# Eight groups of a weight product ahead of the experts in place of five, and a later store of the soft maxima

## The chip, the cores and the metric

One Trainium2 chip, one of its cores. The metric is the device time of one execution in microseconds; the kernel before has a median of 406.53 us in 3 runs.

The core has five engines that run their own instruction streams: TensorE (PE, with its weight loads shown as PEld), VectorE (DVE), ScalarE (ACT), GpSimd (POOL) and SyncE (SP, which issues nearly all transfers here). Matmul results go to eight PSUM banks, all else lies in on-chip tiles or in DRAM.

## What is computed

Three layers follow one another, in float32: a retention attention over 8 batches, 8 heads, 576 positions and 64 features; a soft mixture of 8 experts with 4 slots each over the 4608 tokens; and a bilinear layer.

```python
def _attn_ref(q, k, v):                      # scores weighted by Dmat, then times v
    ...
    ret = scores * Dmat[None, :, :, :]
    return np.matmul(ret, v)

def _moe_ref(x, phi, w1, w2):
    logits = x @ phi                         # 4608 x 32
    d = np.exp(logits - logits.max(0));  d /= d.sum(0) + 1e-09
    slot_input = d.T @ x
    for e in range(E):
        h = np.maximum(slot_input[e] @ w1[e], 0.0)
        slot_out[e] = h @ w2[e]
    ...
    c = np.exp(logits - logits.max(1));  c /= c.sum(1) + 1e-09
    return c @ slot_out

def _moe2_ref(x, w1, w2, w3, w_out):
    a = x @ w1
    b = x @ w2
    h = a * b @ w3
    return h @ w_out
```

w3 and w_out are 64-bit in DRAM, and so are the two projections w1 and w2 of the bilinear layer; the kernel turns them into 32-bit values itself.

## The kernel before

**Stages.** A loop over 36 units of 128 tokens does the attention and, beside it, the logits, running soft maxima over the tokens and the slots' sums. A passage behind it finishes the maxima: the normalisers, and `slotm`, the experts' input. A loop over the 8 experts follows. Behind it the slots' outputs are turned (`acc`, `sot`), multiplied by the two projections (L985), multiplied pairwise (VectorE, L1029 to L1036), and multiplied by W (L1044). The last loop writes 36 blocks of 128 tokens (L1110 to L1125), with coefficients made from the soft maxima over the slots.

**W, the product of the weights.** W = w3 x w_out does not depend on the data, so its matmuls are put wherever `emit_Ws(n)` is called: n groups of three matmuls of 128x512 each (high by high, high by low, low by high part; L557). There are 64 groups, 4 for each of 16 blocks of w3 and 8 for each of 8 blocks of W. A block of w3 is loaded (L472), converted on ScalarE, VectorE and GpSimd (L490 to L516), cast to its high part on ScalarE (L521) and split on GpSimd (L526) into one of three places in `w3p`. A place is written again when its four groups are done. Each eighth group ends a block of W, which is evicted at the next `tick()`: a cast on ScalarE (L565) and a subtraction on VectorE (L566).

**Where the groups stand.** Three and then five behind the attention; in the experts' loop as many as a count that rises with the step lets through (up to 52, and three more in the last expert); three, two and four behind the loop.

**An expert.** `emit_l1(e)`: 32 matmuls (L593) with four tiles of 512 KB of w1. ScalarE makes `hr` (L598), VectorE turns it into `ht` (L605), and `emit_l2(e)`: 16 matmuls (L612) with four tiles of w2. The tiles' places come free with these matmuls, and `load_expert` puts the next loads on SP (L576) into free places. SP issues in program order; each transfer also waits for the one that stands eight before it on SP.

**The passage ahead of the experts.** ScalarE casts two blocks of w3 (L521), each as soon as its place is read for the last time by the product's groups, and then brings `zacc` up to date (L434). VectorE makes `zb` from it (L874) and, behind that, the last sum `acc` (L451). TensorE's matmuls with `zb` (L875) and `acc` (L881) follow, then the first expert's first layer.

**The soft maxima over the slots.** In the experts' loop nine steps (`soft`) fill `et`. `store_expt` writes it to DRAM (`expt`) in 16 transfers on SP (L416), and `load_pairs` reads it back (L624 to L626) into `lga`, `raw` and `vals`, 12 transfers for each of 9 blocks. `pair_prep` makes the coefficients; its first product for the first block is on GpSimd (L638), its cast on ScalarE (L639).

## Time and profile before

| | before |
|---|---|
| median of 3 runs | 406.53 us (404.79 to 406.96) |
| the profiled execution's own time | 406.82 us |
| its span | 405.1 us |
| TensorE busy | 382.5 us (94%) |
| VectorE, ScalarE, GpSimd busy | 260.7, 199.8, 172.1 us (64%, 49%, 42%) |
| moved | 108.75 MB, 268 GB/s in the mean |

TensorE is busy nearly throughout, but that share is a mean over stages with different limits. The views that tell them apart are the chain that ended last, the order of each engine's instructions in time with the idle time ahead of each and what ended it, and short stretches with the clock that TensorE was granted and the share of the transfer engines. Their rows stand further below.

### The profile page before, as it was taken

How to read it: one execution, taken by the hardware profiler on the slowest of the kernel's cores; microseconds unless marked ns; L12 is line 12 of the kernel's file. 1: busy time of each engine (PE TensorE's matmuls, PEld its weight loads, DVE VectorE, ACT ScalarE, POOL GpSimd, SP SyncE). 2: the span in 40 equal slices, each digit the busy share in tenths (PEclk: the TensorE clock that was granted, in tenths of full speed). 3: DMA queues.
4: the chain of work that ended last, by engine and by line, in shares of the span. 5: the costliest groups of instructions: out<-in, count | busy, mean ns of one | idle time of the engine just before them, and what ended most of it. 6: DMA issues, size and time to landing. Idle time of an engine off the chain costs nothing.

```text
span 405.1 us, 10964 instructions
## 1 busy us (share of the span) xinstructions
PE 382.5 (94%) x4447; PEld 286.0 (71%) x4447; DVE 260.7 (64%) x432; ACT 199.8 (49%) x424; POOL 172.1 (42%) x158
## 2 busy tenths in 40 slices
PE   6999988998999998979999898999999999999996
PEld 3888676877878886555565354567877777787774
DVE  3457999998888998426874572179866444455500
ACT  2346695777667785315454322045345445452532
POOL 2632777564264545022643342034734345543520
PEclk9999999999999999989999899999999999999999
DMA  7999898799979888996999999593076998999634
GB/s 234 308 333 322 266 367 299 226 353 391 304 239 331 331 266 301 310 404 243 391 406 407 411 407 409 163 211 77 2 171 154 238 223 229 220 216 235 154 84 104
DMA packets 48211, 108.75 MB, mean 268 GB/s; under 512 B 7584, under 2 KB 10016, under 8 KB 48160
## 3 DMA queue, kind: packets, MB, share of 16 engines
q1 hardware_dynamic: 47008, 107.85, 83.6%
q8 instruction: 35, 0.57, 0.6%
q10 hardware_dynamic: 1152, 0.20, 0.3%
q14 instruction: 16, 0.13, 0.1%
HBM read 97.41 MB, written 10.62 MB: 267 GB/s over the span
## 4 chain that ended last, share of the span: by engine, by line
PE 43%; DMA 7%; DVE 2%; ACT 1%; issue 0%; ACTq 0%; DVEq 0%; SPq 0%
PE bank L1119 9%; PE bank L1121 8%; PE bank L1120 8%; PE bank L557 5%; PE bank L1044 5%; DMA v<-in_ew 3%; DMA kt<-in_ew 3%; PE bank L612 2%; DMA k<-in_ew 2%; PE bank L593 2%; PE bank L1110 2%; PE bank L1074 1%; PE bank L985 1%; DVE w L566 0%; ACT w L565 0%
## 5 line engine op out<-in xcount | busy, mean ns | idle before, releaser
L636 POOL TENSOR_TENSOR cc<-mw_sb,cc 128x512 fp32r<-128x512 f32 x36 | 46.0, 1297 | 56.1 <-ACT cc L635 56.1
L516 POOL TENSOR_TENSOR vals<-vals,msb 128x512 int32<-128x512 int32 x24 | 30.8, 1284 | 57.7 <-DVE vals L490 37.2
L557 PE MATMUL bank<-wop,w3p 128*128 128x512 f32 x192 | 52.0, 414 | 0.0
L557 PEld LDWEIGHTS bank<-wop,w3p 128*128 128x128 f32 x192 | 35.3, 194 | 15.7 <-issue 9.0
L263 DVE TENSOR_TENSOR pm<-scores,msb 128x1024 f32<-128x1024 f32 x31 | 37.8, 1219 | 12.8 <-PE scores L253 12.5
L635 ACT CAST cc<-mw_sb 128x512 fp32r<-128x512 f32 x36 | 22.2, 616 | 43.6 <-DVE mw_sb L634 34.8
L1119 PE MATMUL bank<-w3p,cc 128*128 128x512 f32 x108 | 43.1, 399 | 0.0
L1121 PE MATMUL bank<-w3p,cc 128*128 128x512 f32 x108 | 42.1, 390 | 0.0
L1120 PE MATMUL bank<-w3p,cc 128*128 128x512 f32 x108 | 42.0, 389 | 0.0
L253 PE MATMUL scores<-q,kt 64*128 64x128 f32 x496 | 37.3, 290 | 0.0
L634 DVE TENSOR_TENSOR mw_sb<-lga,raw 128x512 f32<-128x512 f32 x32 | 29.3, 955 | 12.3 <-POOL cc L636 12.1
L282 PE MATMUL output<-pm,v 128*64 128x128 f32 x512 | 35.2, 279 | 1.1 <-issue 1.0
L526 POOL TENSOR_TENSOR w3p<-vals,w3p 128x512 fp32r<-128x512 f32 x16 | 20.5, 1283 | 33.7 <-ACT w3p L521 33.7
L1123 ACT ACTIVATE mw_sb<-bank,rz 128x512 f32<-128x512 f32 x36 | 24.7, 685 | 20.1 <-PE bank L1121 11.3
L516 POOL TENSOR_TENSOR mw_sb<-mw_sb,msb 128x512 int32<-128x512 int32 x16 | 20.4, 1277 | 32.0 <-DVE mw_sb L490 22.4
L253 PEld LDWEIGHTS scores<-q,kt 64*128 64x128 f32 x496 | 31.1, 192 | 3.0 <-issue 1.1
L282 PEld LDWEIGHTS output<-pm,v 128*64 128x64 f32 x512 | 27.4, 136 | 6.3 <-issue 4.5
L192 POOL TENSOR_TENSOR k<-kr,msb 128x512 f32<-128x512 f32 (+1 forms) x30 | 26.3, 897 | 5.3 <-DMA kr<-in_v 3.1
L220 ACT COPY kt<-pair 128x512 f32<-128x512 f32 x26 | 15.3, 587 | 26.0 <-PE pair L219 26.0
L497 ACT ACTIVATE msb<-raw 128x512 int32<-128x512 uint32 x40 | 27.9, 698 | 0.0
L316 PE MATMUL output<-q,st 64*64 64x128 f32 (+1 forms) x512 | 20.1, 268 | 6.5 <-DVE xts L327 4.5
L1119 PEld LDWEIGHTS bank<-w3p,cc 128*128 128x128 f32 x108 | 20.3, 188 | 7.1 <-issue 2.9
(226 smaller groups left out, 777.1 us busy)
## 6 DMA issues: line engine op xcount, KB each, us to landing
q<-in_q SPq DMA_DIRECT2D x20, 512.0 KB, 6.4
raw<-expt SPq DMA_DIRECT2D x36, 256.0 KB, 4.2
kr<-in_v SPq DMA_DIRECT2D x16, 512.0 KB, 6.2
v<-in_v SPq DMA_DIRECT2D x16, 512.0 KB, 6.7
raw<-in_m SPq DMA_DIRECT2D x16, 512.0 KB, 5.9
raw<-in_w SPq DMA_DIRECT2D x16, 512.0 KB, 6.3
out_x<-mw_sb SPq DMA_DIRECT2D x64, 128.0 KB, 2.4
k<-in_ew SPq DMA_DIRECT2D x14, 512.0 KB, 10.1
```

Of the source, the lines that this page charges most:

```text
L192: (nc.vector if first else nc.gpsimd).tensor_tensor(out=Ks[:, :, 0:m, h], in0=K[:, 1 - h, :, 0:m], in1=ktab(c, h)[:, 0:m].unsqueeze(1).uns ...
L253: last = nc.tensor.matmul(out=ps[:, p], lhsT=ktb[u % 2][a, p], rhs=Q[a, :, x, p], start=True, stop=True)
L263: nc.vector.tensor_tensor(out=p_places[u % 2].rearrange("p (g t) -> p g t", g=8), in0=(pair if u == 1 else scores).rearrange("p (g t) -> p ...
L282: last = nc.tensor.matmul(out=xt_view(p)[side(p, h)], lhsT=v_tile(u)[:, 1 - h, x, p], rhs=p_main(u)[:, h, p], start=(block_of(u) == 0 and ...
L497: lambda: nc.scalar.activation(out=p.bitcast(I32), in_=lo, func=ACTF.Copy, scale=2.0 ** -29),
L516: nc.gpsimd.tensor_tensor(out=ti, in0=ti, in1=parts[j % 2].bitcast(I32), op=ALU.add)
L557: nc.tensor.matmul(out=ps, lhsT=x, rhs=y, start=(k8 == 0 and part == 0), stop=(k8 == 7 and part == 2))
L634: eng.tensor_tensor(out=e, in0=x, in1=y[:, m], op=ALU.mult)
L636: nc.gpsimd.tensor_tensor(out=cl[m], in0=e, in1=ch[m], op=ALU.subtract)
L1119: nc.tensor.matmul(out=ob, lhsT=ch[m][:, sl], rhs=gh[m], start=False, stop=False)
L1120: nc.tensor.matmul(out=ob, lhsT=ch[m][:, sl], rhs=gl[m], start=False, stop=False)
L1121: nc.tensor.matmul(out=ob, lhsT=cl[m][:, sl], rhs=gh[m], start=False, stop=(m == 3))
```

## The change

Three groups of the product move from behind the experts' loop to ahead of it: `emit_Ws(5, 0)` becomes `emit_Ws(8, 0)`, the counts in the loop rise by three, so that each step of the loop has as many as before, and the calls of three and two behind the loop become one and one. The store of the soft maxima is called in the last expert instead of behind the last but one, and its first transfer now also waits for the last matmul of the last expert's first layer.

```diff
--- before.py
+++ after.py
@@ -409,14 +409,19 @@
         nc.tensor.transpose(ps[:, 0:128], ee.rearrange("p g s -> p (g s)"), ident)
         nc.scalar.copy(out=L["et"][T // 8][:, T % 8], in_=ps[:, 0:128])
 
-    def store_expt():
+    def after(i, j):
+        tc.add_manual_dep(i.ins, j.ins.name, mybir.DependencyInfo(mybir.DependencyClass.Sync, mybir.DependencyReason.DATA), reason="pace")
+
+    def store_expt(last):
         for T, n in ((0, 8), (8, 1)):
             for g in range(4):
                 for o in (0, 32):
-                    nc.sync.dma_start(
+                    i = nc.sync.dma_start(
                         out=bass.AP(expt.tensor, expt.offset + 512 * (64 * T + o) + 128 * g, [[512, 32], [64 * 512, n], [1, 128]]),
                         in_=L["et"][T // 8][32 * g:32 * g + 32, 0:n],
                     )
+                    if T + g + o == 0:
+                        after(i, last)
 
     def emit_dT(T):
         dd = st[T][0]
@@ -582,7 +587,7 @@
     def pace(behind):
         if waiting and behind is not None:
             for i in waiting.pop(0)():
-                tc.add_manual_dep(i.ins, behind.ins.name, mybir.DependencyInfo(mybir.DependencyClass.Sync, mybir.DependencyReason.DATA), reason="pace")
+                after(i, behind)
 
     hr_of, ht_of = {}, {}
 
@@ -590,7 +595,7 @@
         ps = bank[e % 2]
         for k in range(4):
             for g in range(4):
-                nc.tensor.matmul(
+                last = nc.tensor.matmul(
                     out=ps[32 * g:32 * g + 32, 0:256], lhsT=slotm[:, 128 * e + 32 * k:128 * e + 32 * k + 32],
                     rhs=ew[8 * e + k][:, 256 * g:256 * g + 256], start=(k == 0), stop=(k == 3), skip_group_check=True,
                 )
@@ -598,6 +603,7 @@
         nc.scalar.activation(out=hr, in_=ps[:, 0:256], func=ACTF.Relu)
         hr_of[e] = hr
         free.extend(ew[8 * e:8 * e + 4])
+        return last
 
     def emit_turned(e):
         hr = hr_of[e]
@@ -863,7 +869,7 @@
         free.extend(xt_places)
         load_expert(3)
         run(subs)
-        emit_Ws(5, 0)
+        emit_Ws(8, 0)
         run_copies()
         next_conv(NU)
         run_conv(5)
@@ -926,7 +932,9 @@
         emit_turn(0)
         for e in range(NE):
             load_expert(8)
-            emit_l1(e)
+            last = emit_l1(e)
+            if e == NE - 1:
+                store_expt(last)
             if e == 0:
 
                 free[:] = [t for t in free if not any(t is x for x in ring)]
@@ -939,7 +947,7 @@
                 if t == 1:
                     emit_turned(e)
                 load_expert(8)
-                emit_Ws(max(0, min(52, 9 + (4 * e + t + 1) * 44 // 28) - nW[0]))
+                emit_Ws(max(0, min(55, 12 + (4 * e + t + 1) * 44 // 28) - nW[0]))
                 if e == NE - 1 and t == 1:
                     emit_Ws(3, 0)
                 if t == 2:
@@ -950,9 +958,7 @@
                 while e < NE - 1 and nsoft[0] <= (4 * e + t) * 18 // 28:
                     soft()
                 convert(2 + t % 2)
-            if e == NE - 2:
-                store_expt()
-        emit_Ws(3, 0)
+        emit_Ws(1, 0)
         so = acc
         nc.scalar.copy(out=so[:, 0:256], in_=bank[4][:, 0:256])
         nc.vector.tensor_copy(so[:, 256:512], bank[4][:, 256:512])
@@ -961,7 +967,7 @@
         for k in range(4):
             nc.tensor.matmul(out=pso[:, k], lhsT=so[:, 128 * k:128 * k + 128], rhs=isum, start=True, stop=True)
         nc.vector.tensor_copy(sot, pso)
-        emit_Ws(2, 0)
+        emit_Ws(1, 0)
         tick()
```

TensorE's instructions between the attention and the normalisers; a bank is a PSUM bank, `wop` and `w3p` hold the product's operands, `zb` the normalisers'; in the changed kernel the same code stands five or six lines further down. Before:

```order
L857 MATMUL bank1_2621<-cst_72,nrow_2693 128x1
L440 MATMUL bank4_2624<-xg0_92,dt_2689 32x512 x2
L440 MATMUL bank4_2624<-xg1_93,dt_2689 32x512 x2
L557 MATMUL bank5_2625<-wop_78,w3p_79 128x512 x15
L875 MATMUL bank1_2621<-cst_72,zb_2732 128x32
L881 MATMUL bank3_2623<-ib_2730,acc_75 128x32
```

With the change:

```order
L863 MATMUL bank1_2621<-cst_72,nrow_2693 128x1
L445 MATMUL bank4_2624<-xg0_92,dt_2689 32x512 x2
L445 MATMUL bank4_2624<-xg1_93,dt_2689 32x512 x2
L562 MATMUL bank5_2625<-wop_78,w3p_79 128x512 x15
L562 MATMUL bank2_2622<-wop_78,w3p_79 128x512 x9
L881 MATMUL bank1_2621<-cst_72,zb_2741 128x32
L887 MATMUL bank3_2623<-ib_2739,acc_75 128x32
```

Three groups, nine matmuls into the second block's bank, now stand between the eighth group and the normalisers.

TensorE's instructions from the last expert's second layer (operands `q1`, `v1`, `k0`, `k1` with `ht`) to the two projections (operand `sot`). Before:

```order
L557 MATMUL bank5_2625<-wop_78,w3p_79 128x512 x9
L612 MATMUL bank4_2624<-q1_99,ht_3383 32x512 x2
L612 MATMUL bank4_2624<-v1_102,ht_3383 32x512 x2
L612 MATMUL bank4_2624<-k0_106,ht_3383 32x512 x2
L612 MATMUL bank4_2624<-k1_107,ht_3383 32x512 x2
L557 MATMUL bank5_2625<-wop_78,w3p_79 128x512 x3
L557 MATMUL bank2_2622<-wop_78,w3p_79 128x512 x6
L962 MATMUL bank3_2623<-cst_72,acc_75 128x32 x4
L557 MATMUL bank2_2622<-wop_78,w3p_79 128x512 x6
L985 MATMUL bank7_2627<-mw_sb_77,sot_3413 32x256 x16
L985 MATMUL bank6_2626<-mw_sb_77,sot_3413 32x256 x16
L557 MATMUL bank2_2622<-wop_78,w3p_79 128x512 x12
```

With the change:

```order
L562 MATMUL bank5_2625<-wop_78,w3p_79 128x512 x3
L562 MATMUL bank2_2622<-wop_78,w3p_79 128x512 x6
L618 MATMUL bank4_2624<-q1_99,ht_3392 32x512 x2
L618 MATMUL bank4_2624<-v1_102,ht_3392 32x512 x2
L618 MATMUL bank4_2624<-k0_106,ht_3392 32x512 x2
L618 MATMUL bank4_2624<-k1_107,ht_3392 32x512 x2
L562 MATMUL bank2_2622<-wop_78,w3p_79 128x512 x3
L968 MATMUL bank3_2623<-cst_72,acc_75 128x32 x4
L562 MATMUL bank2_2622<-wop_78,w3p_79 128x512 x3
L991 MATMUL bank7_2627<-mw_sb_77,sot_3419 32x256 x16
L991 MATMUL bank6_2626<-mw_sb_77,sot_3419 32x256 x16
L562 MATMUL bank2_2622<-wop_78,w3p_79 128x512 x12
```

Behind the second layer stand three product matmuls where nine were, and behind the turn of `acc` three where six were.

VectorE's instructions around the transposition of the fourth expert (`ht` from `hr`); `w3` is the fourth evicted block of W, `vals` and `raw` belong to the conversion, `et1` and `rz2` to the soft maxima. Before:

```order
L496 TENSOR_SCALAR vals_82<-vals_82 128x512
L498 TENSOR_SCALAR vals_82<-vals_82 128x512
L490 SCALAR_TENSOR_TENSOR vals_82<-raw_80,vals_82 128x512
L605 STREAM_TRANSPOSE ht_3054<-hr_3038 128x256
L396 TENSOR_REDUCE mx_3062<-bank3_2623 128x4
L397 TENSOR_TENSOR et1_2769<-bank3_2623,mx_3062 128x128
```

With the change:

```order
L407 TENSOR_TENSOR rz2_74<-rz_3029 128x4
L501 TENSOR_SCALAR vals_82<-vals_82 128x512
L571 TENSOR_TENSOR w3_3068<-bank2_2622,w3_3068 128x512
L611 STREAM_TRANSPOSE ht_3071<-hr_3051 128x256
L396 TENSOR_REDUCE mx_3079<-bank3_2623 128x4
L397 TENSOR_TENSOR et1_2778<-bank3_2623,mx_3079 128x128
```

The eviction's subtraction now stands right ahead of this transposition; before, it came eight instructions behind it.

## Rows read from the trace of the kernel before

**Rows 1.** TensorE in order of time: start us, us, instruction [idle before <-releaser]

```profile
171.90 3.72 PE L557 MATMUL bank<-wop,w3p 128*128 128x512 f32 x15
...
177.57 0.41 PE L875 MATMUL bank<-cst,zb 128*128 128x32 f32 x2 [1.96 <-DVE zb L874]
...
180.76 1.93 PE L593 MATMUL bank<-kr,slotm 128*32 128x256 f32 x16
...
187.26 0.62 PE L612 MATMUL bank<-v,ht 128*32 128x512 f32 x2 [0.36 <-DVE ht L605]
```

**Rows 2.** The same view for ScalarE and VectorE, up to the normalisers

```profile
175.48 0.62 ACT L521 CAST w3p<-vals 128x512 fp32r<-128x512 f32 x1 [2.19 <-PE bank L557]
...
176.42 1.10 DVE L874 TENSOR_SCALAR zb<-zacc,beta 128x128 f32<-128x128 f32 x1 [4.89 <-ACT zacc L434]
```

**Rows 3.** 1-us stretches: busy PE PEld DVE ACT POOL, granted clock, transfer share, GB/s

```profile
181.00:182.00 1.00, 1.00 (x12) 0.40 (x8) 0.00 (x0) 0.00 (x0) 0.00 (x0) 0.50 1.03 422
...
188.00:189.00 1.00, 1.00 (x12) 0.13 (x4) 0.97 (x4) 0.03 (x1) 0.60 (x1) 1.00 0.06 20
...
224.00:225.00 1.00, 1.00 (x10) 0.18 (x3) 0.96 (x2) 0.00 (x0) 1.00 (x2) 1.00 1.02 406
...
254.00:255.00 1.00, 1.00 (x12) 0.14 (x4) 0.00 (x0) 0.00 (x0) 0.00 (x0) 1.00 1.12 348
```

**Rows 4.** SP's issues in order of time, behind the hole in the transfers

```profile
188.74 0.38 SPq L576 DMA_DIRECT2D q<-in_ew  x1
```

**Rows 5.** TensorE in order of time: its waits for weights in the experts

```profile
228.96 0.64 PE L593 MATMUL bank<-st,slotm 128*32 128x256 f32 x8 [1.31 <-DMA st<-in_ew]
...
230.24 0.76 PE L593 MATMUL bank<-kt,slotm 128*32 128x256 f32 x8 [0.64 <-DMA kt<-in_ew]
...
250.68 0.64 PE L593 MATMUL bank<-q,slotm 128*32 128x256 f32 x8 [0.65 <-DMA q<-in_ew]
```

**Rows 6.** Chain that ended last: start us, us, what; from second expert

```profile
190.95 1.86 PE bank L593 x32
...
246.34 9.40 DMA k<-in_ew
...
255.79 1.05 PE bank L612 x4
256.84 2.27 PE bank L557 x9
259.11 0.81 PE bank L962 x8
259.92 1.47 PE bank L557 x6
```

**Rows 7.** VectorE in order of time behind the last load: acc, sot

```profile
257.29 0.42 DVE L958 COPY acc<-bank 128x256 f32<-128x256 f32 x1 [4.98 <-ACT acc L957]
...
259.96 0.29 DVE L963 COPY sot<-bank 128x128 f32<-128x128 f32 x1 [2.24 <-PE bank L962]
```

**Rows 8.** In order of time: GpSimd's closest split, TensorE's groups behind it

```profile
217.90 1.28 POOL L526 TENSOR_TENSOR w3p<-vals,w3p 128x512 fp32r<-128x512 f32 x1 [4.43 <-ACT w3p L521]
...
219.32 3.06 PE L557 MATMUL bank<-wop,w3p 128*128 128x512 f32 x12
```

**Rows 9.** In order of time: SP's stores, GpSimd's pair product, its user

```profile
246.86 13.84 SPq L416 DMA_DIRECT2D expt<-et  x16
...
271.06 1.30 POOL L638 TENSOR_TENSOR mw_sb<-lga,vals 128x512 f32<-128x512 f32 x1 [0.88 <-DMA vals<-expt]
...
277.45 0.62 ACT L639 CAST cs<-mw_sb 128x512 fp32r<-128x512 f32 x1
```

**Rows 10.** In order of time: an eviction, the second layer behind it

```profile
243.53 0.59 ACT L565 CAST w<-bank 128x512 fp32r<-128x512 f32 x1
...
244.15 0.69 DVE L566 TENSOR_TENSOR w<-bank,w 128x512 fp32r<-128x512 f32 x1 [3.76 <-ACT w L565]
...
245.25 1.06 PE L612 MATMUL bank<-k,ht 128*32 128x512 f32 x8 [0.24 <-DVE ht L605]
```

## The prediction

> **What bounds the kernel now.** I read the views in this order: the chain that ended last, the order of TensorE's instructions in time with the idle time ahead of each, the stretches of 1 us with granted clock and transfer share, and last the engines that release TensorE. From the end of the span backwards TensorE's matmuls are the chain, but for one short passage on VectorE ahead of the pair products, as far as the last expert; ahead of that the chain leaves TensorE for the loads of the experts' weights [rows 6]. So there are three stretches with different limits.
>
> Between attention and experts TensorE is the limit, and it stands still for 1.96 us ahead of the sum of the normalisers [rows 1]. The wait is not for the 15 matmuls before it. Those end at 177.57 - 1.96 = 175.61; ScalarE's second cast into w3p runs from 175.48, the factor zacc stands behind that cast on ScalarE, and VectorE starts zb at 176.42 and ends at 177.52 [rows 2]. Right after the gap the clock stands at its lower level, 1.2 GHz: granted 0.50 [rows 3]. The first expert's 32 matmuls run from 179.91 (slotm) to the 15 product matmuls, which start 3.71 ahead of the end that [rows 1] shows at 187.26 - 0.36 = 186.90, so at 183.19: 3.28 us. Another expert's 32 take 1.86 us at 2.4 GHz [rows 6].
>
> In the experts the transfers are the limit: they move 406 GB/s at a share of 1.02 [rows 3], TensorE waits for weights at 228.96, 230.24 and 250.68 (1.31, 0.64 and 0.65 us, [rows 5]), and the last load runs from 246.34 to 255.74 [rows 6]. Ahead of that the transfers had a hole, a share of 0.06 at 188 [rows 3], because the next loads need places that the first expert's second layer gives free: SP issues them from 188.74 on, when that layer has ended [rows 4].
>
> Behind the last load TensorE is the limit again: 1.05 of the last second layer, nine product matmuls (2.27), the turn of the slots (0.81), six more (1.47), then the two projections [rows 6].
>
> **Three groups ahead of the experts.** Nine matmuls at 3.72/15 = 0.248 us [rows 1] are 2.23. They follow the 15 and need nothing new: the third block of w3p was split before attention ended, and the wait of zacc's cast is for the eighth group, which keeps its place. So they run from 175.61 to 177.84, zb is ready at 177.52, and the normalisers' matmuls start 0.27 us later than before. Their next user on the path is the sum of the slots, which waits for acc on VectorE anyway, behind zb; I take 0 for this, 0.27 at most.
>
> What is gained is the clock. With the gap filled I expect the first expert's 32 matmuls to take 1.86 in place of 3.28: 1.42 us. Below it is bounded by 0 (the clock falls all the same) and above by 1.42. The way to the end is through SP. The first expert's cast, its transposition, the second layer and the frees follow those 32 matmuls, so the load at 188.74 and a load of w3 just ahead of it [rows 4] go out 1.42 us earlier, into the hole. Behind it the transfers run full, as at 224 [rows 3], so the last load lands 1.42 us earlier, at 254.32. TensorE and the transfers shift together, and the waits in the experts stay about as they are. **Term 1: -1.42 us.**
>
> **Three groups fewer behind the last load.** Before, L985 starts at 259.92 + 1.47 = 261.39. Now three matmuls follow the second layer: 256.84 + 0.74 = 257.58. The six that are gone also covered two copies: ScalarE's and VectorE's halves of acc, one behind the other; VectorE's ends at 257.29 + 0.42 = 257.71 [rows 7]; with 0.05 from VectorE to TensorE the turn starts at 257.76 and TensorE waits 0.18. It takes 0.81, to 258.57. VectorE's copy of sot, 0.04 later and 0.29 long [rows 7], is done at 258.90, under the three matmuls that end at 259.31. So L985 starts at 259.31, 2.08 us earlier. The bounds: 2.23 if the copies cost nothing, 1.6 if each of the two hand-overs costs a quarter of a microsecond more. **Term 2: -2.08 us.** What follows (the projections, the pair products, 108 groups of output) depends on these and shifts whole.
>
> **The inside of the experts' loop.** The product's groups run three ahead, with as many per step. The closest split of a w3 block ends on GpSimd at 217.90 + 1.28 = 219.18, and its first user is now where the last of the four groups from 219.32 was, 221.6 [rows 8]: 2.4 us to spare, so no wait there. Evictions, casts and one load of w3 on SP move by a step or two. That load now stands ahead of four loads of weights: the same bytes, and a wait of one load (1.3 us) may move from 229 forward to 223. I cost these at 0: the transfers cover them, and each would cost what it takes if TensorE became the limit there (fourth rival).
>
> **The later store.** Its first transfer now waits for the last first-layer matmul, which ends at 250.68 + 0.64 = 251.32 [rows 5], in place of 246.86 [rows 9]. Behind it on SP stand the other 15 stores and the loads of the pairs, no load of weights. Before, the 16 took 13.84 us to issue, because each waits for the transfer eight before it; the later ones are held by the last weights until 255.74, then and now. GpSimd's first pair product waits for the loads, 271.06 to 272.36, and its user on ScalarE comes at 277.45 [rows 9]. Of these 5.09 us term 2 takes 2.08, which leaves 3.01. If only the first few stores move, the cost is 0, which I take; if all move by the full 4.46, it is 1.45. On the other side, transfers fall to 348 GB/s while stores run among the last loads [rows 3]; if this slowed the loads, 2.7 us x (1 - 348/406) = 0.39 would come back. The Trainium skill ("DMA: Bandwidth & Descriptors", section Queues, rings and completion order) speaks against that gain: each transfer engine takes its ring in order, so a store issued behind a load takes nothing from it. By it the sum stays; by the row it would be 402.9. Which holds, no row of before tells.
>
> **The sum.** The profiled execution took 406.82 us (span 405.1), 0.29 above the median of 406.53. 406.82 - 1.42 - 2.08 = 403.3 us.
>
> **The rivals.** (B) The clock falls all the same. For: between 177.8 and 179.9 TensorE has only small matmuls and short waits, and the phase of the clock's falls against the program may differ. Against: this fall came behind the largest gap before the experts. Term 1 goes, 404.7. The Trainium skill ("TensorE: Matmul & The Clock Gate", section A second HAM failure mode: psum-queue depth-cycling) sides with this rival: frequent short idling between groups of matmuls is enough to swing the clock.
>
> (C) The store comes late by its full 4.46 us and GpSimd's pairs hold up ScalarE: 403.3 + 1.45 = 404.8. Against it speaks that the later stores were held by the weights already.
>
> (D) The change doesn't fill the gap. If the release of ScalarE's cast comes from the end of all eight groups, and not of the five, zacc moves 2.23 us back and the same wait opens behind them: 406.82 + 2.23 - 2.08 = 407.0. Against: the second cast starts at 175.48 [rows 2], as the last of the 15 matmuls leaves and not later, so the eighth group itself releases it.
>
> (E) The other side, slower: the evictions. Each is a cast of 0.59 and a subtraction of 0.69, and seven now stand inside the loop. Where one stands right ahead of the transposition on VectorE, the second layer waits, 0.24 at 245.25 [rows 10]; now this is so in the fourth expert, before in the second and seventh. If TensorE waited for all seven in full, 7 x 1.28 = 8.96, less 1.31 + 0.64 + 0.65 = 2.60 of waits that exist, it would be 6.36 - 3.50 = +2.86: 409.7. It decides from 2.6 + 3.5 + 2.0 = 8.1 us of such waits on. Against: the second place of before cost only 0.24.
>
> **How the numbers follow.** Forecast 0.62; B 0.15; C 0.08; D 0.08; E 0.07. About 0.5% is what a measurement of this kernel can tell from no change: 404.5 to 408.6 is the same. The forecast and a third of B and C are faster, 0.70; the rest of B and C with D is the same, 0.23; E is slower, 0.07. The range reaches from 402.0 (term 2 at 2.23 and the stores' 0.39 make 402.8; the runs of before spread by 2.2 us, of which I leave 0.8) to 405.3, past B and C; D and E, 0.15, are left out.
>
> **What would show it.** Right: no idle time above 0.3 us ahead of the normalisers, the granted clock at 1.00 through the first expert, its 32 matmuls in some 1.9 us, the load q at about 187.3, the last weights at about 254.3, and from their landing to L985 3.6 us in place of 5.65. Wrong: a clock of 0.50 at 180, a last load still at 255.7, GpSimd waiting for the pairs' loads with ScalarE idle behind it, or a second layer that waits on VectorE in most experts.

## The result and the profile after

The changed kernel takes 402.81 us (median of 7 runs, 400.67 to 403.26) against 406.01 for the kernel before beside it, a ratio of 0.9907 with a 95% interval of 0.9879 to 0.9936. Timed a second time it took 402.23 us, ratio 0.9901 (0.9876 to 0.9926). The prediction was 403.3 us, within 402.0 to 405.3. The ratio is estimated from the runs and is not the quotient of the two medians, which lie 3.20 us apart; where this text says "by the ratio", it is 1 - ratio times the median of the kernel before, here 3.8 us (2.6 to 4.9). The profiled execution's span went from 405.1 to 401.1 us.

TensorE in order of time from the attention's end, the counterpart of [rows 1] (start us, us, instruction, idle before and releaser; the code stands five or six lines further down now):

```profile
170.77 5.73 PE L562 MATMUL bank<-wop,w3p 128*128 128x512 f32 x24
176.45 0.41 PE L881 MATMUL bank<-cst,zb 128*128 128x32 f32 x2
177.11 1.22 PE L887 MATMUL bank<-ib,acc 128*128 128x32 f32 x12 [0.25 <-DVE acc L456]
...
178.78 0.64 PE L598 MATMUL bank<-ew,slotm 128*32 128x256 f32 x8 [0.19 <-DVE slotm L892]
...
180.65 3.69 PE L562 MATMUL bank<-wop,w3p 128*128 128x512 f32 x15
184.71 0.62 PE L618 MATMUL bank<-v,ht 128*32 128x512 f32 x2 [0.38 <-DVE ht L611]
```

The 24 matmuls run into the normalisers with no idle time. From the start of the product to the normalisers it is 176.45 - 170.77 = 5.68 us; before it was 177.57 - 171.90 = 5.67 [rows 1], so the three groups cost nothing here. The reason is on VectorE, the counterpart of [rows 2]: zb is ready when the 24th matmul ends.

```profile
175.27 1.13 DVE L880 TENSOR_SCALAR zb<-zacc,beta 128x128 f32<-128x128 f32 x1 [4.86 <-ACT zacc L439]
```

The first expert's 32 matmuls now take 180.65 - 178.78 = 1.87 us; they took 3.28. The stretches of 1 us, as in [rows 3] (busy PE, PEld, DVE, ACT, POOL, granted clock, transfer share, GB/s): the clock stays at 1.00, 2.4 GHz, and the hole in the transfers remains, but 2 us earlier and less deep (a share of 0.49 in its emptiest stretch, 0.06 before).

```profile
180.00:181.00 1.00, 1.00 (x18) 0.46 (x10) 0.00 (x0) 0.22 (x1) 0.00 (x0) 1.00 1.03 422
...
186.00:187.00 1.00, 1.00 (x11) 0.43 (x4) 1.00 (x1) 0.06 (x1) 1.00 (x2) 1.00 0.49 143
```

SP's issues behind that hole, the counterpart of [rows 4] (q, v, k, pm, st, kt and the like are names of the places that the experts' tiles are loaded into): the load q goes out at 186.18 in place of 188.74. Of these 2.56 us, 1.12 lie ahead of the normalisers (177.57 against 176.45: the attention ran faster in this execution), and 1.44 are the first expert's. The second row is a load of w3, which comes back to us below.

```profile
186.18 0.38 SPq L581 DMA_DIRECT2D q<-in_ew  x1
...
190.90 0.33 SPq L477 DMA_DIRECT2D raw<-in_w  x1
```

TensorE's waits for weights in the experts, the counterpart of [rows 5], are 0.57 to 0.64 us each; the longest of before was 1.31. There are five of them ahead of the first layers, 3.09 us together, three of which are shown; before, four made 2.82. So there is not less waiting, only no long wait.

```profile
228.32 0.64 PE L598 MATMUL bank<-kt,slotm 128*32 128x256 f32 x8 [0.63 <-DMA kt<-in_ew]
...
237.29 0.64 PE L598 MATMUL bank<-v,slotm 128*32 128x256 f32 x8 [0.64 <-DMA v<-in_ew]
238.56 0.64 PE L598 MATMUL bank<-k,slotm 128*32 128x256 f32 x8 [0.62 <-DMA k<-in_ew]
```

The end of the experts in the chain that ended last (start us, us, what), the counterpart of [rows 6], and under it VectorE's two copies, that of [rows 7]:

```profile
244.09 9.71 DMA k<-in_ew
253.85 1.05 PE bank L618 x4
254.90 0.90 PE bank L562 x3
255.80 0.81 PE bank L968 x8
256.61 0.78 PE bank L562 x3
257.38 1.91 PE bank L991 x32
```

```profile
255.35 0.42 DVE L964 COPY acc<-bank 128x256 f32<-128x256 f32 x1 [3.68 <-ACT acc L963]
256.64 0.29 DVE L969 COPY sot<-bank 128x128 f32<-128x128 f32 x1 [0.87 <-PE bank L968]
```

From the last four matmuls of the second layer to the projections it is 257.38 - 253.85 = 3.53 us in this view; before, it was 261.39 - 255.79 = 5.60. The turn starts 0.03 us behind VectorE's copy of acc, whose end is 255.77. Behind the projections nothing changed: from their first row in TensorE's order to the end of the span it is 143.8 us in both traces.

The stores and what follows them, in order of time, the counterpart of [rows 9]:

```profile
249.52 9.69 SPq L419 DMA_DIRECT2D expt<-et  x16
259.25 0.43 SPq L630 DMA_DIRECT2D lga<-expt  x1
...
269.26 1.31 POOL L644 TENSOR_TENSOR mw_sb<-lga,vals 128x512 f32<-128x512 f32 x1 [3.09 <-DMA vals<-expt]
...
273.44 0.62 ACT L645 CAST cs<-mw_sb 128x512 fp32r<-128x512 f32 x1
```

The stores begin 2.66 us later, but take 9.69 in place of 13.84 us to issue. GpSimd's pair product waits 3.09 us for its loads; its result is there at 270.57, and the cast on ScalarE comes 2.87 later.

Inside the experts' loop the groups that run three ahead, and with them the evictions, do show (TensorE, the counterpart of [rows 10]): the second layer of the third expert waits 0.77 us for its transposition.

```profile
203.42 1.06 PE L618 MATMUL bank<-q,ht 128*32 128x512 f32 x8 [0.77 <-DVE ht L611]
```

That of the fourth expert, which the prediction named, waits 0.30.

The balance of the two traces has four pieces: up to the normalisers -1.12 us, from there to the last four matmuls of the second layer 77.40 in place of 78.22, -0.82, from those to the projections -2.07, and 0 behind. Together that is the -4.0 us of the spans.

So the second term came out, and of the first only 0.8 us reached the end in this execution. Whether the rest was lost to something the change does, or is the spread of one execution, is what most of the experiments are about.

### The profile page after: what moved, and what is told of

It is laid out like the page before. It is cut to its first block, busy times and chain, and to the rows that moved or that the text cites. A ratio compares the mean times of both kernels' runs of the same rounds, so it can differ in the third digit from the quotient of the medians.

```text
span 401.1 us, 10962 instructions
## 1 busy us (share of the span) xinstructions
PE 379.6 (95%) x4447; PEld 284.2 (71%) x4447; DVE 259.1 (65%) x432; ACT 199.9 (50%) x424; POOL 172.7 (43%) x158
## 4 chain that ended last, share of the span: by engine, by line
PE 36%; DMA 11%; DVE 3%; ACT 2%; issue 1%; POOL 1%; SPq 0%; ACTq 0%; POOLq 0%
PE bank L1125 9%; PE bank L1127 8%; PE bank L1126 8%; PE bank L1050 5%; DMA k<-in_ew 5%; DMA v<-in_ew 3%; DMA kt<-in_ew 3%; PE bank L1116 2%; PE bank L562 2%; PE bank L618 1%; PE bank L1080 1%; DMA raw<-expt 1%; DVE vals L495 1%; PE bank L598 1%; PE bank L991 0%
## 5 line engine op out<-in xcount | busy, mean ns | idle before, releaser
L562 PE MATMUL bank<-wop,w3p 128*128 128x512 f32 x192 | 50.4, 405 | 0.0
L562 PEld LDWEIGHTS bank<-wop,w3p 128*128 128x128 f32 x192 | 34.2, 188 | 14.9 <-issue 8.7
```

The costliest lines, as they stand in the source:

```text
L562: nc.tensor.matmul(out=ps, lhsT=x, rhs=y, start=(k8 == 0 and part == 0), stop=(k8 == 7 and part == 2))
```

## The experiments

All were timed in the same way, each beside runs of the kernel before. The table holds what each left. "Gap" is the idle time ahead of the normalisers, "first expert" its 32 matmuls, "to the last layer" the time from the normalisers to the last four matmuls of the last second layer, "tail" from those to the projections, all four in us from TensorE's order in the profiled execution. "Clock" is the mean granted clock over the whole program and all runs of the kernel, so a fall of the clock elsewhere counts in it too.

| kernel | gap | clock | first expert | to the last layer | tail | ratio (95% interval) |
|---|---|---|---|---|---|---|
| before | 1.96 | 0.992 | 3.28 | 78.22 | 5.53 | |
| later store alone | 1.96 | 0.994 | 3.16 | 77.70 | 5.56 | 0.9992 (0.9974 to 1.0011) |
| shorter tail alone | 1.96 | 0.993 | 3.57 | 79.15 | 3.46 | 0.9952 (0.9933 to 0.9971) |
| gap half filled | 1.05 | 0.993 | 3.57 | 78.80 | 5.54 | 0.9983 (0.9961 to 1.0004) |
| gap filled, nothing moved | 0 | 0.998 | 1.86 | 76.70 | 5.54 | 0.9960 (0.9933 to 0.9986) |
| eight ahead, old tail | 0 | 0.998 | 1.86 | 77.11 | 5.54 | 0.9984 (0.9962 to 1.0005) |
| the same again | 0 | 0.998 | 1.87 | 77.67 | 5.54 | 0.9967 (0.9947 to 0.9988) |
| the change without the store | 0 | 0.999 | 1.86 | 76.71 | 3.46 | 0.9936 (0.9912 to 0.9960) |
| the change | 0 | 0.999 | 1.87 | 77.40 | 3.46 | 0.9907 (0.9879 to 0.9936) |
| the same again | 0 | 0.998 | 1.86 | 76.69 | 3.47 | 0.9901 (0.9876 to 0.9926) |
| gap filled, shorter tail | 0 | 0.999 | 1.87 | 76.84 | 3.47 | 0.9908 (0.9876 to 0.9941) |
| change, evictions late | 0 | 0.999 | 1.87 | 76.51 | 3.47 | 0.9894 (0.9851 to 0.9938) |
| change, second layer early | 0 | 0.998 | 1.86 | 77.60 | 3.47 | 0.9887 (0.9844 to 0.9930) |
| both | 0 | 1.000 | 1.86 | 77.94 | 3.45 | 0.9896 (0.9852 to 0.9940) |

### The parts of the change

**The groups without the store.** The change as it is, but the store is called behind the last expert but one, and waits for nothing new.

```diff
+                    if last is not None and T + g + o == 0:
+                        after(i, last)
...
             if e == NE - 2:
-                store_expt()
+                store_expt(None)
```

> The change without its later store: the groups are moved as in the change, the store stands where it stood before and waits for nothing new. My theory: the store is worth nothing, so this gives what the whole change gives, about 402.8 us, a ratio near 0.991; from the last load's landing to L985 3.6 us. Rival, the store clears the way for the last loads: the time is up to 0.4 us above the change's, 403.2, and the transfer rate falls below 406 GB/s ahead of the last landing as it did before. A second rival, the later store costs: it is 0.5 us or more below the change's time.

403.24 us, ratio 0.9936. This is 2.6 us less than before, with an interval from 1.6 to 3.6. The expected 0.991 lies just outside that interval, and the time is the 403.2 that the first rival named, so by the times alone the later store could be worth something together with the groups. The trace doesn't show it: 76.71 and 3.46 us, and 143.8 behind, as in the second trace of the change. Nor does the kernel with the gap filled and the tail shortened, further below, which has the store of before and a ratio of 0.9908.

**The store alone.** The kernel before with `store_expt` in the last expert and the wait for its last first-layer matmul.

```diff
             if e == NE - 1:
+                store_expt(last)
```

> The kernel before with the later store alone, no group moved. My theory: 406.0 us, a ratio of 1.000; the gap of 1.96 us ahead of the normalisers, the clock of 0.50 behind it and 5.65 us from the last landing to L985 all stay. Rival, the store clears the way: 0.4 us less, 405.6. Rival, the store comes late: up to 1.4 us more, 407.4, with ScalarE waiting for GpSimd's first pair product.

405.42 us, ratio 0.9992: no difference that can be told, though the interval alone would leave room for 0.39 us. What speaks against it is the way of the last loads: from the start of SP's row with the last two loads of weights to the last four matmuls it is 11.50 us before and with the groups alone, 11.51 with the later store alone, and 11.44 in both traces of the whole change. The rate does fall ahead of the landing, with the later store too: 302 GB/s from 253 to 254 with the store alone, where before had 348. So a falling rate is no sign that the loads are slowed. The Trainium skill ("DMA: Bandwidth & Descriptors", section Queues, rings and completion order) says that each transfer engine takes its ring in order, though a later transfer may finish its write before an earlier one; that a store therefore takes nothing from a load ahead of it was the prediction's own conclusion. These figures agree with it, and the possible 0.39 us that the prediction took from the falling rate was not there.

**The tail alone.** Five groups ahead as before, three more inside the loop, one and one behind it.

```diff
-                emit_Ws(max(0, min(52, 9 + (4 * e + t + 1) * 44 // 28) - nW[0]))
+                emit_Ws(max(0, min(55, 9 + (4 * e + t + 1) * 44 // 28 + sum(4 * e + t >= k for k in (11, 15, 19))) - nW[0]))
-        emit_Ws(3, 0)
+        emit_Ws(1, 0)
-        emit_Ws(2, 0)
+        emit_Ws(1, 0)
```

> Five groups ahead of the experts as before, three more groups inside the experts' loop (in the third to sixth expert), three fewer behind the last load; the store as before. My theory: the gap of 1.96 us and the clock of 0.50 behind it stay, the waits for weights in the loop take the three groups in, and L985 comes 2.08 us earlier behind the last landing: 403.9 us, a ratio near 0.995. Rival, TensorE is the limit inside the loop: the last load lands later by what the groups take there, 2.2 us, and the time is 406.

404.12 us, ratio 0.9952: 1.95 us of 405.88, between 1.2 and 2.7, for a second term of 2.08. TensorE's order at the end:

```profile
255.68 1.05 PE L612 MATMUL bank<-k,ht 128*32 128x512 f32 x4 [0.22 <-DMA k<-in_ew]
256.66 0.97 PE L557 MATMUL bank<-wop,w3p 128*128 128x512 f32 x3
257.46 0.97 PE L962 MATMUL bank<-cst,acc 128*128 128x32 f32 x8
258.27 0.94 PE L557 MATMUL bank<-wop,w3p 128*128 128x512 f32 x3
259.14 3.23 PE L985 MATMUL bank<-mw_sb,sot 128*32 128x256 f32 x56
```

It is the tail of the changed kernel, 3.46 us, though the gap ahead of the normalisers is there and the first expert runs at the lower clock.

**Eight ahead, the tail as before.** The three groups are taken from the loop.

```diff
-        emit_Ws(5, 0)
+        emit_Ws(8, 0)
-                emit_Ws(max(0, min(52, 9 + (4 * e + t + 1) * 44 // 28) - nW[0]))
+                emit_Ws(max(0, min(52, 12 + (4 * e + t + 1) * 41 // 28) - nW[0]))
```

> Eight groups ahead of the experts, three fewer inside the loop, behind the last load and the store as before. My theory: the gap is filled and the clock stays at its upper level, the load q goes out 1.4 us earlier after the normalisers than before, of which 0.8 to 1.4 us reach the last landing; 5.65 us from there to L985 stay: 404.6 to 405.2 us, a ratio of 0.9965 to 0.998. Rival, the transfers of the experts take whatever the clock gives back: the last landing keeps its distance to the end of the attention and the time is 406.

404.86 us, ratio 0.9984: 0.65 us by the ratio (-0.2 to 1.5), where term 1 says 1.42, which the interval still holds. The clock stayed up (first expert 1.86 us), and still no more than 1.1 us are gone between the normalisers and the last layer. Here, as in the changed kernel, evictions stand ahead of a conversion on VectorE, and the load of w3 behind it (190.90 above) goes out later against its neighbours than before. Theory A, which the next expectations test, came from this: the move of the evictions takes back a part of the clock's gain.

### Is it the clock

**The gap filled, nothing moved.** The kernel before with nine extra matmuls in the gap.

```diff
         emit_Ws(5, 0)
+        for _ in range(9):
+            nc.tensor.matmul(out=bank[2], lhsT=block(w3p, 2)[:, 0:128], rhs=woh[:, 0:512], start=True, stop=True)
```

> The kernel before with nine extra matmuls of 128x512 (2.23 us) in the gap ahead of the normalisers, into a bank that nobody reads then; their result is used by nobody, and the 64 groups of the product stay where they are. So the gap is filled, and no eviction moves. If the clock is what the gap costs: granted clock 1.00 there, the first expert's 32 matmuls in 1.87 us in place of 3.28. Theory A (the gain is real, and in the changed kernel a part of it is lost to the evictions that stand ahead of a conversion and hold up a load of w3 on SP): here no eviction has moved, so the last load lands 1.2 to 1.4 us earlier in the program, ratio 0.9965 to 0.997. Rival B (the transfers lose the gain by themselves, whatever the evictions do): as with eight groups ahead and the tail as before, 0.4 to 0.7 us, ratio 0.998 to 0.999. Rival C (other work behind the passage needs the same 2.2 us, so extra work there is not free): 1.000 or above.

404.24 us, ratio 0.9960, though TensorE does 2.2 us more work. TensorE's order, and one stretch of 1 us (the view of the order ends at 186.5 us, so its last row has 14 of 15 matmuls):

```profile
176.97 2.20 PE L868 MATMUL bank<-wop,w3p 128*128 128x512 f32 x9
179.12 0.41 PE L877 MATMUL bank<-cst,zb 128*128 128x32 f32 x2
...
181.45 0.64 PE L593 MATMUL bank<-ew,slotm 128*32 128x256 f32 x8 [0.19 <-DVE slotm L888]
...
183.31 3.48 PE L557 MATMUL bank<-wop,w3p 128*128 128x512 f32 x14
```

```profile
182.00:183.00 1.00, 1.00 (x27) 0.56 (x20) 0.00 (x0) 0.00 (x0) 0.00 (x0) 1.00 1.02 406
```

From the normalisers to the last layer it is 76.70, 1.52 less than before. So what the gap costs is the clock behind it, and the gain reaches the last layer: 1.6 us by the ratio (0.6 to 2.7). That interval also holds the 0.998 of rival B; it is the trace that speaks for the whole 1.42. The traced execution itself took 406.83 us, because its attention ended late; only the stretch behind the normalisers is compared.

**The gap half filled.** The same with four extra matmuls.

> The kernel before with four extra matmuls in the gap in place of nine; their result is used by nobody. A wait of about 0.97 us for zb stays. If a shorter gap is enough to keep the clock: granted clock 1.00 behind it, the first expert's 32 matmuls in 1.87 us and a ratio like that of the filled gap, 0.996 to 0.997. If any gap of about a microsecond lets the clock fall: 3.2 to 3.3 us, ratio 1.000.

405.58 us, ratio 0.9983: not told from no change. The wait that is left is 1.05 us, and the clock falls behind it as behind 1.96:

```profile
173.70 1.07 PE L868 MATMUL bank<-wop,w3p 128*128 128x512 f32 x4
175.82 0.41 PE L877 MATMUL bank<-cst,zb 128*128 128x32 f32 x2 [1.05 <-DVE zb L876]
```

```profile
177.00:178.00 1.00, 1.00 (x11) 0.83 (x9) 0.00 (x0) 0.00 (x0) 0.00 (x0) 0.50 1.04 414
...
182.00:183.00 1.00, 1.00 (x6) 0.84 (x3) 0.00 (x0) 0.79 (x2) 0.00 (x0) 0.50 0.84 246
...
184.00:185.00 1.00, 1.00 (x6) 0.82 (x5) 0.29 (x1) 0.59 (x2) 0.00 (x0) 1.00 1.01 340
```

The first expert's 32 matmuls take 3.57 us, all at the lower clock, and the fall does not end with them: the granted clock is 0.50 in all six stretches of 1 us from 177 to 183. Before, it was 0.50 only in the two from 180 to 182 ([rows 3] show one), with 0.71 and 0.58 in their neighbours, and 1.00 again from 183 on:

```profile
183.00:184.00 1.00, 1.00 (x12) 0.68 (x5) 0.00 (x0) 0.66 (x2) 0.00 (x0) 1.00 0.58 197
```

So the product's matmuls behind the first expert ran slowly too. The load pm, which waits for a place that the second expert's second layer gives free, goes out 197.03 - 175.82 = 21.21 us behind the normalisers with the gap half filled, 197.76 - 177.57 = 20.19 before:

```profile
197.03 0.33 SPq L576 DMA_DIRECT2D pm<-in_ew  x1
```

```profile
197.76 0.33 SPq L576 DMA_DIRECT2D pm<-in_ew  x1
```

The shorter tail alone, with the whole gap of 1.96, has such a long fall as well (0.50 from 177 to 183, pm at 21.17), the later store alone a short one (0.50 from 180 to 183, pm at 20.03). With the gap filled pm stands at 18.75. A fall thus cost 1.3 to 1.4 us up to there in two traces and 2.4 to 2.5 in the other two, and the length of the gap did not decide which.

The column of the clocks agrees in the mean: 0.992 to 0.994 wherever the gap was left, 0.998 to 1.000 wherever it was filled. It does not hold for every execution. A fall like that of before takes 0.004 off the mean (3.4 us at half the clock in 405), and of the 106 timed executions with a whole or half gap three have 0.998 or 0.999, which leaves no room for one. They took 403.77, 403.24 and 404.04 us, 1.4 to 2.6 less than the medians of their kernels (405.79 twice, 405.42). None of the three was traced, but they point the same way as the filled gap, and without an extra matmul.

Half a gap saved nothing that can be told: in its trace the clock fell all the same, and the interval holds no gain as well as one of 1.6 us.

### Where the rest of the first term went

**The evictions behind the conversion.** The changed kernel, but in the loop each eviction runs behind its step's conversion.

```diff
+            if not inside[0]:
+                run(evicts)
-            run(evicts)
...
+                late = evicts[:]
+                evicts.clear()
...
                 convert(2 + t % 2)
+                run(late)
```

> The changed kernel with one difference: in the experts' loop each eviction of a block of W runs behind the conversion of its step in place of ahead of it. Theory A: the conversion of a w3 block, which in the changed kernel waited behind the eviction on VectorE at 189.4 to 190.0, frees its place 0.7 us earlier, the load of w3 goes out on SP at about 190.1 in place of 190.9, the waits of the second layers for the transposition (0.77 and 0.30) go, and the time falls by 0.5 to 0.8 us below that of the changed kernel: 402.0 to 402.3, ratio 0.989 against the kernel before. Rival B (the transfers lose the gain by themselves): as the changed kernel, 402.8, ratio 0.9907. Rival C: a cast that now comes later on ScalarE holds the next groups' bank, and it is slower by up to a microsecond.

402.46 us, ratio 0.9894: theory A's 0.5 to 0.8 us below the changed kernel is not ruled out, but neither is no difference. Of the two waits for the transposition the one of 0.30 us is gone, but 0.48 of the 0.77 is still there, so the evictions were not all of it. The load of w3 goes out 13.55 us behind the normalisers in place of 14.45, as meant, and the last layer comes at 76.51.

**The changed kernel again.**

> The changed kernel once more, unaltered, for a second trace. In its first trace the last second layer began to end 77.40 us behind the normalisers (before: 78.22), 0.6 less than term 1 says. Theory F (the 0.6 us is the spread of one execution's transfers in the first 30 us behind the hole): this distance comes out anywhere from 76.5 to 77.6, and the ratio is 0.989 to 0.993. Theory A (the evictions that moved ahead of a conversion hold up a load of w3 and so cost 0.6 us each time): the distance is 77.3 to 77.5 again.

402.23 us, ratio 0.9901, and in its trace 76.69 us to the last layer, though the load of w3 goes out as late as in the first trace, 14.44 us behind the normalisers. Theory A falls with this, since it asked for 77.3 to 77.5 again: the same order of instructions gives 77.40 and 76.69. The change without the store says the same, with a load of w3 at 14.44 and 76.71, against 76.70 where no eviction was moved and that load went out at 13.11. Further down all are even again: the load pm goes out 18.75 or 18.76 us behind the normalisers in all four, since it needs a place that the second expert's second layer gives free. SP's waits around pm, st and kt (in total, times, longest), in the second trace of the change and then in the first:

```profile
SPq L581 <- PE bank L618: 1.9, 2, 1.4
```

```profile
SPq L581 <- DMA v<-in_ew: 0.8, 1, 0.8
SPq L581 <- DMA q<-in_ew: 0.7, 1, 0.7
...
SPq L581 <- PE bank L618: 0.2, 1, 0.2
```

The first trace falls behind here. In it SP stood before transfers that were not done, and st and kt went out 1.28 us apart; in the other three it was 0.42. Against the second trace it is 1.12 us late at kt, and 0.69 is left from the load q on. What slowed the transfers in that one execution is not settled.

**Eight ahead, old tail, again.**

> The kernel with eight groups ahead of the experts, three fewer in their loop and the tail as before, once more, unaltered. Theory F: the distance from the normalisers to the last second layer is 76.5 to 77.6 and not 77.11 again, and the ratio is nearer to that of the filled gap, 0.996 to 0.997. Theory A: 77.0 to 77.4, ratio 0.998 to 0.999.

404.31 us, ratio 0.9967, near the filled gap's 0.9960. Its trace has 77.67 us to the last layer; theory F allowed up to 77.6 and theory A named 77.0 to 77.4, so neither distance came; the ratio is the one of theory F. The load pm goes out at 18.53 in both traces of this kernel, with st and kt 0.42 apart, so what this trace lost, it lost further on. The two sets of times, 0.65 (-0.2 to 1.5) and 1.3 us (0.5 to 2.2) by the ratio, leave room for the full 1.42 and for a part of it.

**The gap filled and the tail shortened, no group ahead.** Both edits from above.

> The kernel before with nine extra matmuls in the gap, whose result is used by nobody, and with three product groups fewer behind the last load; the three stand in the experts' loop. So both terms without a group moved ahead. If the two terms add: 1.4 + 2.0 = 3.4 to 3.5 us, ratio 0.9913, though this kernel does 2.2 us more work. If the three more groups in the loop cost what the transfers don't cover: 0.993 to 0.996.

401.96 us, ratio 0.9908 (expected 0.9913 if the terms add): 3.7 us by the ratio (2.4 to 5.0), as much as the change brings, with no product group moved ahead of the experts, the store as before and 2.2 us more work on TensorE. So the two terms are enough for the change's gain, and they add, as far as intervals of more than 1 us to either side can tell.

### An earlier end of the hole

**The first expert's second layer in its first step.** The changed kernel, with the transposition and the second layer of the first expert two steps earlier.

```diff
+                if e == 0 and t == 0:
+                    emit_turned(e)
-                if t == 1:
+                if e and t == 1:
                     emit_turned(e)
...
-                if t == 2:
+                if t == (2 if e else 0):
```

> The changed kernel with one difference: the first expert's transposition and second layer stand in its first step and not in its second and third, so that the second layer no longer comes behind product groups and frees its four tiles sooner. The transfers have a hole there until these tiles come free. If the hole is what sets the last landing (the transfers run full from then on), the load q goes out some 2 us earlier than at 186.2, the last load lands 1.2 to 2 us earlier in the program, and the time is 400.8 to 401.6, ratio 0.986 to 0.988. If the place where the loads start no longer matters (the second layers of the later experts, or the rate near the end, set the landing), 402.8 as the changed kernel. If the second layer waits for the transposition on VectorE by over 0.5 us and the clock falls again, 403.5 or more.

402.48 us, ratio 0.9887 (0.9844 to 0.9930): the interval holds the changed kernel's 0.9907 and also the 0.986 to 0.988 of the first expectation, so the trace has to decide. The loads do go out earlier, and then SP stands before a load of w3. SP in order of time, and what it waited for from 180 to 200 us (in total, times, longest):

```profile
180.84 2.91 SPq L581 DMA_DIRECT2D q<-in_ew  x2
184.25 0.33 SPq L581 DMA_DIRECT2D v<-in_ew  x1
184.67 0.77 SPq L581 DMA_DIRECT2D q<-in_ew  x1
185.66 5.48 SPq L477 DMA_DIRECT2D raw<-in_w  x2
191.24 0.38 SPq L581 DMA_DIRECT2D v<-in_ew  x1
```

```profile
SPq L477 <- DVE vals L495: 5.9, 3, 4.8
```

The three loads behind the hole, q, v and q, are out some 2.5 us earlier against the normalisers; the second load of w3 waits 4.8 us for VectorE's conversion, and what stands behind it goes out as in the changed kernel: pm at 194.91, 18.39 us behind the normalisers in place of 18.76. The last layer comes at 77.60, no earlier than in the changed kernel. So in this trace the end of the hole alone does not set the last load.

**Both.** With the evictions behind the conversions as well.

> The changed kernel with both: the evictions behind the conversion of their step, and the first expert's second layer in its first step. If the two act on the same thing (the start of the transfers behind the hole) their gains add: 400.2 to 401.0, ratio 0.985 to 0.987. If the transfers lose such gains by themselves, it is that of the better of the two, 401.5 to 402.8.

402.79 us, ratio 0.9896: the second expectation, 401.5 to 402.8, came. The gains do not add; there is none to be told. No version here beats the changed kernel by more than the measurement's uncertainty.

## Why the prediction was right, step by step

**Term 1, -1.42.** The three groups fill the gap, the clock stays, and the first expert takes 1.87 us: 1.41 less, as said. Its way to the end was right as well, but no one trace shows it to better than half a microsecond: 0.82 and 1.53 us in the two traces of the change, 1.52 with the gap merely filled; by the ratio 1.6 (0.6 to 2.7) for the filled gap, 0.65 (-0.2 to 1.5) and 1.3 (0.5 to 2.2) for eight groups ahead. The mean of the ten traces with a filled gap is 77.12 us to the last layer, that of the four with a gap 78.47: 1.35, while the single ones overlap (76.51 to 77.94 and 77.70 to 79.15).

That 1.42 is so near has some luck in it. It is the price of the fall in the one trace that the prediction read, where the clock was back up when the first expert ended. In two of the four traces with a gap the fall went on into the product's matmuls and had cost 2.4 to 2.5 us by the load pm. The trace of before also had a second fall, at 230 to 234 us (the stretch at 231 is shown at the end), in which nine of the product's matmuls took 3.77 us in place of 2.34. It is no part of the gain: from the kt matmuls to the last layer it is 255.79 - 230.24 = 25.55 us before and 253.85 - 228.32 = 25.53 with the change, where more waiting for weights took its place (2.46 us, against 0.87 before).

The step "through SP" was told too simply. The earlier loads at the end of the hole are not enough (the second layer two steps earlier); all of TensorE has to come earlier, because the place for pm comes free with the second expert's second layer. The clock's gain does that, since it moves everything behind it.

**The normalisers, 0 to 0.27.** 0.01 was measured.

**Term 2, -2.08.** 2.07 was measured; the tail alone gave 1.95 (1.2 to 2.7) by the ratio.

**The loop inside, 0.** Evictions do hold up a transposition here and there (0.77 and 0.30 us) and a load of w3 (1.3 us), and none of it reached the end, as 76.71 and 76.69 us to the last layer with it and 76.70 without it show. No matmul waited for a split of w3. The fourth rival, E, named the right cause and one of the two places (the fourth expert, 0.30; the 0.77 is in the third), but not a price that counts.

**The store, 0.** 0.9992 (0.9974 to 1.0011) alone. The first store went out 2.66 us later, the pair product had 2.87 us to spare where the sum left 3.01, and the 0.39 us of a possible gain for the last loads were not there.

**The sum.** 406.82 - 3.50 = 403.3 stood for one execution. The first trace of the change gave -4.0, of which 1.12 belong to an attention that ran faster in it, the second 405.1 - 401.4 = -3.7. By the ratio it was 3.8 us (2.6 to 4.9) and 4.0 (3.0 to 5.0), by the medians 3.2 and 3.6; the sum of 3.50 lies between. That 402.81 us came so near to 403.3 owes something to where the sum began: with an execution of 406.82 us, while the median beside the change was 406.01. Of the rivals, B did not come: in none of the ten traces with a filled gap does the first expert take more than 1.87 us. The Trainium skill ("TensorE: Matmul & The Clock Gate", section A second HAM failure mode: psum-queue depth-cycling) tells of another kernel in which frequent short idling between groups of matmuls made the clock swing. This is not seen here: waits of 0.25, 0.19 and 0.38 us follow one another from 177 to 185 in the changed kernel, and the granted clock stays at 1.00. Whether more of them in closer succession would do it was not tried. C, D and E did not come either.

## What to carry to other kernels

A wait of one or two microseconds ahead of a stretch that is bound by TensorE can cost twice, once as a wait and once as a lower clock behind it. Look at the granted clock right behind each such gap, and fill the whole of it with work that is needed anyway: half a gap saved nothing that could be told here. Work that stands behind the last arrival on the critical path is worth its full length if it can go to a place where the engine waits, less what it covered (here 2.23 - 2.08 = 0.15 us of two copies). And before a part of a gain is explained from a single pair of traces, the same kernel should be traced twice.

## What the runs showed that was not expected

A wait of 1.05 us was followed by a fall of the clock, but not every wait of this size was. In the experts, the kernel before waited 1.31 and 0.64 us for weights [rows 5], and the clock was down behind it; with the gap half filled it waited there 1.24 and 0.63 us, and the clock stayed. It also stayed behind 1.30 and 0.63 us with the later store alone, 1.32 and 0.63 with the gap filled, and a single 1.55 with eight groups ahead. The stretches of 1 us behind the two, before and then gap half filled:

```profile
231.00:232.00 1.00, 1.00 (x3) 0.81 (x4) 0.00 (x0) 0.96 (x3) 0.00 (x0) 0.50 1.02 406
```

```profile
231.00:232.00 1.00, 1.00 (x8) 0.79 (x7) 0.86 (x2) 0.11 (x1) 1.00 (x1) 1.00 1.05 418
```

So a wait near a microsecond brings the clock down in one execution and not in another; the gap ahead of the normalisers did it in all four traces that have one, while the three executions with 0.998 and 0.999, named above, say that it need not. What decides it, and how long the clock stays down, is not settled.

The same instructions, executed twice, differ by more than the terms at stake: the way from the normalisers to the last layer took 77.40 and 76.69 us for the change, and the normalisers started between 174.91 and 179.12 us in traces whose code up to the end of the attention is the same. In the latest of them, the filled gap's, the clock had also been down once in the attention:

```profile
113.00:114.00 1.00, 1.00 (x13) 1.00 (x12) 0.44 (x1) 1.00 (x4) 0.42 (x1) 0.50 0.17 59
```
